# First four chunks' query and key products moved to head layout by TensorE selections, first six chunks' heads placed in the MLP's layout in PSUM

## The chip, the cores and the metric

The kernel runs on one core of a Trainium2 chip. The metric is the device time of one execution, in microseconds, from the first to the last instruction of the program and what lies around them. A core has TensorE (PE in the profile; PEld is its weight load), VectorE (DVE), ScalarE (ACT), GpSimd (POOL), SyncE (SP), whose queue starts all DMA transfers here, and 16 DMA engines. Matmuls write to PSUM, which has eight banks of 512 float32 columns.

## What is computed

Three parts follow one another: an attention in the form of a complex linear recurrence, a first MLP, and a second, gated MLP, all in float32.

```python
# q, k, v, a_re, a_im: (4, 8, 768, 48): batch, heads, sequence, head width
mag = sqrt(a_re**2 + a_im**2); scale = minimum(mag, 0.999) / (mag + 1e-6)
for t in range(768):                       # S is complex, 48 x 48 for each head
    S = a[t][:, None] * S + outer(k[t], v[t])
    y[t] = q[t] @ real(S)
x = y as (3072, 384)                       # token, head * 48 + column
g = log(1 + exp(x @ w_in)); x = g @ w_out  # 384 -> 2048 -> 384
out = ((x @ w1) * (x @ w2)) @ w3 @ w_out2  # 384 -> 1024 -> 1024 -> 384
```

Weights arrive as 64-bit numbers and are turned into float32 on the chip.

## The kernel before

**Chunks.** The 3072 tokens are cut into 24 chunks `u` of 128 tokens, six to a batch entry; `j` is a chunk's number within its entry. A chunk is worked on with features across the partitions: 384 features are G = 3 groups of 128 partitions, and head `h` takes features 48h to 48h + 47, so that heads 2 and 5 straddle two groups. `norm` (line 451) limits the size of `a`; `scan` (line 516) forms running products of `a` over pairs of chunks, in `P`; `inv` (line 576) forms the query product (`qkp(u, 0, ...)`) and the key product (`qkp(u, 1, ...)`), complex, in one tile `qkp` that has one buffer.

**From groups to heads.** The matmuls of the attention need each head's 48 features on partitions of their own, real parts on 0 to 47 and imaginary parts on 64 to 111: the tile `rs`, one for even and one for odd chunks. Step `s6` of `inv` (line 602) gets there through DRAM: it stores `qkp` to `pd[u]` and loads two halves of it back.

**Heads.** `mm` (line 615) does the rest of a chunk: `kt` turns the key products (transposes `ktp`, copied to `kT`), `sc` makes the scores of four heads in one PSUM bank (masked by VectorE into `am`), and `heads` (line 641) the outputs: `yp` takes, for each head, the state of the chunk before (`S` with `rs`; not where `j` is 0) and the present chunk (`v` with `am`), 48 columns wide, an even head on PSUM partitions 0 to 47 and an odd one on 64 to 111. `stp` is the new state. Two ScalarE copies bring `yp` to a tile `y`, which has one buffer.

**To the MLP's layout.** The MLP wants 384 features on KC = 3 tiles of 128 partitions, full to the last. The array `ROW` (line 65) gives each feature its row: heads 0 to 5 stay where they are, two to a tile, and the 48 columns of heads 6 and 7 fill the free partitions 48 to 63 and 112 to 127 of the three tiles, 16 columns each. Six small DMAs `y<-y` move these columns. Step `x` (line 680) then copies `y` to the block's input `xh` (and its rest to `xl`), or to `x` for the first two blocks.

**Blocks.** The first MLP runs over blocks of tokens: block 0 is chunk 0, block 1 chunks 1 and 2, block 2 chunks 3 to 5, and each later block three chunks. A block has 16 steps `f`: `s1` (line 850) makes `s` from `x`, ScalarE and VectorE make `g` from it, and `s2a` adds it into three banks `acc`. Blocks 0 and 1 use float32 weights, which arrive as raw pieces `wr` from `wio` (`w_load`, line 771; two loads to a piece) and are converted by ScalarE (`wtop`) and VectorE (`w_piece`, line 789) while block 0 runs. Later blocks use the weights and inputs split in two parts (`ww..h`, `ww..l`, `xh`, `xl`). Ahead of all this, `early` multiplies two weights of the second MLP (`wpa`, from `w3t` and `wo2`). Chunks of the next block are interleaved with the steps of a block. The second MLP (`pa`, `pb`, `bg`) follows when all blocks are done.

**PSUM.** Three banks are `acc`; the other five (`S1B = ATT = 5`, `ATAG = "s1"`) are shared by `s`, `ktp`, `sc`, `yp`, `stp` and others.

**Order.** Nothing is run as written: every operation is recorded by `Plan` (from line 79) with a cost and a latency, and `flush` (line 314) sorts them all by list scheduling, forwards and backwards in 16 rounds, one of them with noise from a fixed seed, and takes the best round. Each engine then works through its own list in that order; so does SP with the DMAs. `together` (line 225) keeps a group of matmuls in one piece. All recorded operations carry line 202 in the profile, and are told apart by their tiles.

Of the kernel before, what the change touches and what calls it, by code (L numbers as in the profile page):

```python
# [11 lines left out]
F32 = mybir.dt.float32  # L12
# [10 lines left out]
P = 128  # L23
B, H, SEQ, D = 4, 8, 768, 48
DM = H * D
NT = B * SEQ
T = 128
NCH = NT // T
CPB = SEQ // T
G = DM // P  # L30
# [3 lines left out]
KC = DM // P  # L34
NB = 384
# [5 lines left out]
HB = 5  # L41
# [4 lines left out]
YB = 1  # L46
VB = 1
# [9 lines left out]
CVS = 10  # L57
LEAD = 0
RATE = 340
ROUNDS = 16  # L60
SEED = 214
NBA = NT // NB
# [15 lines left out]
class Plan:  # L78
# [50 lines left out]
    def cost(self, eng, op, outs, ins):  # L129
        n = max(self.free_size(x) for x in (*outs, *ins))  # L130
        if eng == "SP":
            size = 2 if outs[0].dtype == I16 else 4
            for _, n in outs[0].ap:
                size *= n
            rate = 270 if hasattr(ins[0].tensor, "tag_meta") else RATE
            cost = max(650 if n < 512 and self.on_chip(ins[0]) else 475, size / rate)
# [177 lines left out]
    def flush(self):  # L314
# [15 lines left out]
        noise, best = Random(SEED), None  # L330
        for i in range(ROUNDS):
            start, _ = self.run(after, before, dict.fromkeys(before, 0.0), key, {})
# [25 lines left out]
def fused(ctx: ExitStack, tc: tile.TileContext, a_in, qk_in, v_in, wio, w12, w3t, wo2, q, k, v, a_re, a_im, outT):  # L358
    nc = tc.nc
    plan = Plan(tc)  # L360
    V, A, PE, GP, SP = plan.V, plan.A, plan.PE, plan.GP, plan.SP
# [15 lines left out]
    sp = fast.enter_context(tc.tile_pool(name="sp", bufs=2))  # L377
    ps = fast.enter_context(tc.tile_pool(name="ps", bufs=1, space=PSUM))
    ap = fast.enter_context(tc.tile_pool(name="ap", bufs=1))
# [3 lines left out]
    ident = cp.tile([P, P], F32, name="ident")  # L383
# [4 lines left out]
        out=mask, in_=mask, compare_op=ALU.is_ge, fill=0.0, base=0, pattern=[[1, T]], channel_multiplier=-1  # L388
# [23 lines left out]
    c = [dict() for _ in range(NCH)]  # L412
# [7 lines left out]
    def pst(tag, bufs, shape, name):  # L420
        return ps.tile(shape, F32, tag=tag, bufs=bufs, name=name)

    def att_ps(shape, name):
        return pst(ATAG, ATT, shape, name)
# [14 lines left out]

    def load_v(u):  # L440
        s = c[u]
        s["v"] = ap.tile([P, DM], F32, tag="v", bufs=VB, name=f"v{u}")
        SP.dma_start(s["v"], v_in[u])

    def half(u):
        return c[u // R]["P"][:, :, :, (u % R) * T : (u % R + 1) * T]

    def gt(x):
        return x.rearrange("p (g t) -> p g t", t=T)
# [112 lines left out]
    def qkp(u, i, f):  # L562
# [4 lines left out]
            op=ALU.mult,  # L567
        )

    rsw = [ap.tile([P, H * 2 * T], F32, tag=f"rs{i}", name=f"rs{i}") for i in range(2)]  # L570
    rs = [t[0 : 64 + D].rearrange("p (h q t) -> p h q t", h=H, q=2) for t in rsw]
    kT = ap.tile([P, H, 64 + D], F32, tag="kT", name="kT")
# [3 lines left out]
    def inv(u):  # L576
        s = c[u]

        def s1():
            s["n2"] = ap.tile([P, 2, GT], F32, tag="n2", name=f"n2{u}")  # L580
            A.activation(out=s["n2"].rearrange("p c (g t) -> p c g t", t=T), in_=half(u), func=AF.Square)

        def s2():
            n = s["n2"]
            V.tensor_tensor(out=n[:, 0], in0=n[:, 0], in1=n[:, 1], op=ALU.add)
            if u % CPB == CPB - 1:
                A.copy(pend[:, u // CPB], gt(n[:, 0])[:, :, T - 1])
            A.activation(out=n[:, 1], in_=n[:, 0], func=AF.Ln, bias=eps_p)
            A.activation(out=n[:, 1], in_=n[:, 1], func=AF.Exp, scale=-1.0)

        def s3():
            s["qkp"] = ap.tile([P, 2, G, 2, T], F32, tag="qkp", bufs=QKB, name=f"qkp{u}")
            qkp(u, 0, s["qk"][:, 0])

        def s4():
            n = s["n2"]
            V.tensor_tensor(out=n[:, 0], in0=n[:, 1], in1=s["qk"][:, 1], op=ALU.mult)

        def s5():
            qkp(u, 1, s["n2"][:, 0])  # L600

        def s6():
            s["rs"] = rs[u % 2]
            SP.dma_start(
                pd[u].rearrange("(m p) n -> p m n", p=P), s["qkp"].rearrange("p c g q t -> p (c g) (q t)")
            )
            for ri in range(2):
                SP.dma_start(
                    s["rs"][ri * 64 : ri * 64 + D].rearrange("d h q t -> d h (q t)"),
                    pd[u][ri * DM : (ri + 1) * DM].rearrange("(h d) n -> d h n", d=D),  # L610
                )

        return [s1, s2, s3, s4, s5, s6]

    def mm(u):
        s = c[u]
        j = u % CPB
        steps = []

        def kt(ri):  # L620
            def f():
                pt = att_ps([P, G, P], f"ktp{u}_{ri}")
                for g in range(G):
                    PE.transpose(pt[:, g], s["qkp"][:, ri, g, 1], ident)
                A.copy(kT[:, :, 64 * ri : 64 * ri + D], pt.rearrange("p g n -> p (g n)").rearrange("p (h d) -> p h d", d=D))

            return f

        def sc(hh):
            def f():  # L630
                pt = att_ps([P, 4, T], f"sc{u}_{hh}")
                for i in range(4):
                    h = hh * 4 + i
                    PE.matmul(pt[:, i], s["rs"][:, h, 1], s["rs"][:, h, 0], start=True, stop=True)
                am = ap.tile([P, 4, T], F32, tag="am", bufs=AMB, name=f"am{u}_{hh}")
                s[f"am{hh}"] = am
                V.tensor_tensor(out=am, in0=pt, in1=mask.unsqueeze(1).to_broadcast([P, 4, T]), op=ALU.mult)

            return f

        def heads(state):

            s["yp"] = att_ps([P, H // 2, T], f"yp{u}")
            pt = att_ps([P, DM], f"stp{u}") if state else None
            with plan.together():
                for pr in range(H // 2):
                    for prev in (True, False) if j else (False,):
                        for r in range(2):
                            h = 2 * pr + r
                            e = slice(h * D, (h + 1) * D)  # L650
                            w, m = (c[u - 1]["S"], s["rs"][:, h, 0]) if prev else (s["v"], s[f"am{h // 4}"][:, h % 4])
                            PE.matmul(
                                s["yp"][64 * r : 64 * r + D, pr], w[:, e], m,
                                start=prev or j == 0, stop=not prev,
                            )
                for h in range(H if state else 0):
                    for ri in range(2):
                        PE.matmul(
                            pt[64 * ri : 64 + D * ri, h * D : (h + 1) * D], kT[:, h, 64 * ri : 64 + D * ri],
                            s["v"][:, h * D : (h + 1) * D], start=True, stop=True,  # L660
                        )
            s["y"] = ap.tile([P, H // 2, T], F32, tag="y", bufs=YB, name=f"y{u}")
            for r in range(2):
                A.copy(s["y"][64 * r : 64 * r + D], s["yp"][64 * r : 64 * r + D])
            for k in range(KC):
                for r in range(2):
                    SP.dma_start(
                        s["y"][64 * r + D : 64 * (r + 1), k],
                        s["y"][64 * r + 16 * k : 64 * r + 16 * (k + 1), KC],
                    )  # L670
            if not state:
                return
            pt = pt[0 : 64 + D]
            s["S"] = ap.tile([64 + D, DM], F32, tag="S", bufs=2, name=f"S{u}")
            if j == 0:
                A.copy(s["S"], pt)
            else:
                V.tensor_tensor(out=s["S"], in0=pt, in1=c[u - 1]["S"], op=ALU.add)

        def x():  # L680
            bi, c0 = block_of(u)
            if c0 == 0:
                if bi < NATIVE:
                    xt[bi] = (sp.tile([P, KC, NB], F32, tag="xh", bufs=XB, name=f"x{bi}"), None)
                else:
                    xt[bi] = tuple(
                        sp.tile([P, KC, NB], F32R, tag=t, bufs=XB, name=f"{t}{bi}") for t in ("xh", "xl")
                    )
            d = slice(c0, c0 + T)
            xh, xl = xt[bi]  # L690
            if bi < NATIVE:
                A.copy(xh[:, :, d], s["y"][:, 0:KC])
            else:
                split(xh[:, :, d], xl[:, :, d], s["y"][:, 0:KC])

        steps = []
        if j < CPB - 1:
            steps += [kt(0), kt(1)]
        steps += [sc(0), sc(1), lambda: heads(j < CPB - 1), x]
        return steps  # L700

    att_end = {}
    groups = []
    u = 0
# [6 lines left out]
    for us in groups:  # L711
        n = len(us)
# [245 lines left out]
    for bi in range(nblk):  # L958
        last = bi == nblk - 1
        t0, n = BLOCKS[bi]  # L960
        if not last:
            start = att_pos[0]
# [87 lines left out]
    for bi in range(NBB):  # L1050
        gq = {}
        for f in range(FB):
# [6 lines left out]
            while ncheck[0] < min(NCK, NCK * it // nit):  # L1059
                src, n = cks[ncheck[0]]  # L1060
                r = raw3(src, n, f"ckr{ncheck[0]}")
# [4 lines left out]
    for i, n in enumerate(("min", "max")):  # L1066
        V.tensor_reduce(
            out=wlim[:, i : i + 1], in_=bst[n], axis=mybir.AxisListType.X, op=getattr(ALU, n)
        )
    okp = ap.tile([P, DM], F32, tag="v", bufs=VB, name="okp")  # L1070
    c0 = 0
    for src, lim, op in (
# [5 lines left out]
        n = src.shape[1]  # L1078
# [243 lines left out]
```

## Time and profile before

| | us |
|---|---|
| median of three executions | 947.0 (946.98 to 948.58) |
| profiled execution | 949.9 |
| its span, first to last instruction | 948.2 |
| TensorE busy in it | 889.4 (94%) |
| VectorE busy | 729.9 (77%) |
| ScalarE busy | 538.5 (57%) |
| GpSimd busy | 6.8 (1%) |

Busy times are read against the stretch that they lie in: an engine can be full in one stretch and have room in the next. In a profile line, `out<-in` are tiles without their numbers; a matmul of float32 has two instructions; `[4.0 <-ACT xh]` is idle time of the engine ahead of an instruction and what ended it. PEclk is the granted clock of TensorE: 1.00 is 2.4 GHz and 0.50 is 1.2 GHz.

### The profile page before, as it was taken

The page shows a single profiled execution, that of the slowest core. Times are in us where ns is not written, and L with a number is a line of the kernel's source. Part 1 is how long each engine was busy: PE and PEld are TensorE (multiplying, and loading weights), DVE is VectorE, ACT ScalarE, POOL GpSimd, SP SyncE. Part 2 cuts the span into 40 slices and gives each one's busy share as a digit, 9 for nine tenths or more (in the row PEclk, how much of TensorE's full clock was granted, in tenths as well). Part 3 has the DMA queues.
Part 4 walks back from the last instruction along what each step waited for, and adds up shares of the span by engine and source line. Part 5 has one row for each costly group of instructions (what it writes and reads, how often), then busy time and mean ns, then how long its engine had stood idle before and what let it go on. Part 6 is the DMA issues. An engine that isn't in the chain of part 4 may idle for free.

```text
span 948.2 us, 15624 instructions
## 1 busy us (share of the span) xinstructions
PE 889.4 (94%) x5673; PEld 800.3 (84%) x5673; DVE 729.9 (77%) x1591; ACT 538.5 (57%) x1096; POOL 6.8 (1%) x15
## 2 busy tenths in 40 slices
PE   3957779989999999999999999999999999999996
PEld 2536768889999999999999999998878787888885
DVE  6899889999999999899989755599888786222221
ACT  6566885678687689587785655773221323231322
POOL 2000000000000000000000000000000000000000
PEclk9986889999999999999999999999999999999999
DMA  9999866154737455563654435247787774000001
GB/s 346 324 280 279 252 184 146 55 148 113 164 101 153 121 128 114 134 161 61 191 135 130 119 96 132 76 136 243 236 261 237 242 230 145 1 33 1 34 1 37
DMA packets 89127, 141.74 MB, mean 149 GB/s; under 512 B 8273, under 2 KB 60625, under 8 KB 89041
## 3 DMA queue, kind: packets, MB, share of 16 engines
q1 hardware_dynamic: 89040, 140.66, 52.8%
q8 instruction: 46, 0.75, 0.3%
q14 instruction: 41, 0.33, 0.1%
HBM read 109.56 MB, written 29.88 MB: 147 GB/s over the span
## 4 chain that ended last, share of the span: by engine, by line
PE 69%; DMA 13%; DVE 11%; ACT 3%; issue 3%; SPq 1%; DVEq 0%; ACTq 0%
PE acc L202 25%; PE s L202 20%; PE pa L202 6%; PE pb L202 6%; PE sc L202 4%; PE yp L202 3%; DMA ckr<-w3t 3%; DMA ckr<-wio 3%; DMA wr<-wio 3%; DVE ck L202 2%; PE wpa L202 2%; DMA pd<-qkp 2%; DVE P L202 2%; PE stp L202 1%; DVE tm L202 1%
## 5 line engine op out<-in xcount | busy, mean ns | idle before, releaser
L202 DVE TENSOR_TENSOR tm<-P 128x90 f32<-128x90 f32 (+3 forms) x240 | 144.6, 616 | 1.5
L202 ACT ACTIVATE e<-e 128x384 f32<-128x384 f32 (+2 forms) x288 | 135.8, 487 | 2.7
L202 DVE TENSOR_TENSOR bg<-pa,bg 128x512 f32<-128x512 f32 x48 | 33.0, 688 | 91.8 <-PE pa L202 81.5
L202 ACT ACTIVATE e<-s 128x384 f32<-128x384 f32 (+2 forms) x144 | 64.6, 451 | 54.0 <-PE s L202 50.8
L202 ACT CAST bgg<-bg 128x512 fp32r<-128x512 f32 x48 | 29.8, 621 | 114.7 <-DVE bg L202 114.7
L202 DVE SCALAR_TENSOR_TENSOR g<-s,e 128x384 f32<-128x384 f32 (+2 forms) x144 | 73.6, 515 | 24.5 <-ACT e L202 24.4
L202 DVE TENSOR_TENSOR P<-tm 128x45 f32<-128x45 f32 (+11 forms) x304 | 87.2, 344 | 1.6
L202 ACT COPY bg<-pb 128x512 f32<-128x512 f32 x48 | 28.2, 587 | 85.2 <-PE pb L202 78.4
L202 DVE TENSOR_TENSOR gl<-g,gh 128x384 fp32r<-128x384 f32 x112 | 62.1, 559 | 5.8 <-ACT gh L202 5.1
L202 ACT CAST gh<-g 128x384 fp32r<-128x384 f32 x112 | 56.7, 507 | 16.1 <-DVE g L202 11.5
L202 PE MATMUL sc<-rs 112*128 112x128 f32 x384 | 55.1, 286 | 7.3 <-DMA rs<-pd 7.3
L202 PEld LDWEIGHTS sc<-rs 112*128 112x128 f32 x384 | 53.2, 201 | 8.7 <-issue 7.8
L202 DVE CUSTOM_DVE_ANT_0 ck<-ckr 128x384 f32<-128x384 f32 x80 | 43.4, 542 | 21.6 <-DMA ckr<-w3t 9.7
L202 PE MATMUL wpa<-wo,w 128*128 128x384 f32 x128 | 43.2, 499 | 14.3 <-DVE w L202 14.3
L202 PE MATMUL s<-x,w 128*128 128x128 f32 (+1 forms) x192 | 40.8, 363 | 13.7 <-ACT x L202 8.2
L202 PE MATMUL acc<-bgg,bwp0h 128*128 128x512 f32 x144 | 50.8, 391 | 1.7 <-ACT bgg L202 1.3
L202 PEld LDWEIGHTS wpa<-wo,w 128*128 128x128 f32 x128 | 24.9, 196 | 31.5 <-DVE w L202 14.5
L202 PE MATMUL acc<-bgg,bwp2h 128*128 128x512 f32 x144 | 49.2, 392 | 1.2 <-DVE bgg L202 0.8
L202 PEld LDWEIGHTS s<-x,w 128*128 128x128 f32 x192 | 33.7, 218 | 17.5 <-ACT x L202 8.6
L202 DVE TENSOR_TENSOR bgg<-bg,bgg 128x512 fp32r<-128x512 f32 x48 | 33.0, 688 | 16.3 <-ACT bgg L202 16.3
L202 DVE TENSOR_REDUCE lims<-ck 128x1 f32<-128x384 f32 x80 | 43.1, 538 | 2.3
L202 PE MATMUL yp<-am,v 128*48 128x128 f32 x384 | 36.3, 279 | 2.0 <-ACT nt L202 2.0
(372 smaller groups left out, 2308.5 us busy)
## 6 DMA issues: line engine op xcount, KB each, us to landing
pd<-qkp SPq DMA_DIRECT2D x24, 768.0 KB, 4.5
rs<-pd SPq DMA_DIRECT2D x48, 384.0 KB, 6.2
ckr<-wio SPq DMA_DIRECT2D x32, 384.0 KB, 3.8
wr<-wio SPq DMA_DIRECT2D x32, 383.8 KB, 7.3
a<-a_in SPq DMA_DIRECT2D x24, 384.0 KB, 3.7
qk<-qk_in SPq DMA_DIRECT2D x24, 384.0 KB, 3.8
w12r<-w SPq DMA_DIRECT2D x16, 384.0 KB, 3.3
ckr<-w SPq DMA_DIRECT2D x16, 384.0 KB, 3.6
```

The costliest lines, as they stand in the source:

```text
L202: getattr(engine.unit, op)(*args, **kw)
```

## The change

For chunks 0 to 3 (`PICK = 4`), the trip of the query and key products through DRAM gives way to matmuls with selection matrices. `picks` holds, for each head and each group that it lies in (10 pairs), a 128 x 64 matrix of zeros and ones, cut from the identity. `pick(i)` multiplies the query (i = 0) or key (i = 1) product with them, the real part to PSUM partitions 0 to 63 and the imaginary part to 64 to 127, four heads to a bank, and ScalarE copies partitions 0 to 111 to `rs`. It is called as soon as the product in question is there.

For chunks 0 to 5 (`PLACE = 6`), the matmuls of `yp` write the MLP's layout at once. `v` now holds heads 0 to 5 padded with zeros to 64 columns each, then heads 6 and 7 (480 columns instead of 384, for all chunks). For tile k and half r, a first matmul writes 64 rows from head 2k + r; a further one, with weights `ext` of 64 columns whose first 48 are zero and whose last 16 are columns 16k to 16k + 15 of head 6 + r, adds the other head's columns to the rows 48 to 63. The same is done for the state's part where there is one (`ext[1]`, from `S`). ScalarE fills the 16 columns of `ext` for each chunk. `y` is then the PSUM tile itself, and the two copies and the six moves fall away. From chunk 6 on the old way stays, with `vcols` naming the padded columns. `ext` and `picks` lie in buffers of the tiles `gh` and `gl`, which block 2 is the first to use otherwise.

```diff
+PICK = 4
+PLACE = 6
+VW = 6 * 64 + 2 * D
...
-        s["v"] = ap.tile([P, DM], F32, tag="v", bufs=VB, name=f"v{u}")
+        s["v"] = ap.tile([P, VW], F32, tag="v", bufs=VB, name=f"v{u}")
...
+    ext = [sp.tile([P, NB], F32, tag="gh", bufs=HB, name=f"ext{i}") for i in range(2)]
+    for t in ext:
+        GP.memset(t, 0.0)
+    ext = [t.rearrange("p (r k n) -> p r k n", r=2, k=KC) for t in ext]
+    picks = [sp.tile([P, NB], F32, tag="gl", bufs=HB, name=f"pick{i}") for i in range(2)]
+    sels = {}
+    for i in range(2):
+        GP.memset(picks[i], 0.0)
+    for h in range(H):
+        for g in range(h * D // P, ((h + 1) * D - 1) // P + 1):
+            p0 = max(h * D, g * P)
+            n = min((h + 1) * D, (g + 1) * P) - p0
+            i, c0 = divmod(len(sels) * 64, NB)
+            sels[h, g] = picks[i][:, c0 : c0 + 64]
+            GP.tensor_copy(
+                out=picks[i][:, c0 + p0 - h * D : c0 + p0 - h * D + n], in_=ident[:, p0 - g * P : p0 - g * P + n]
+            )
...
+        def pick(i):
+            s["rs"] = rs[u % 2]
+            for hh in range(2):
+                pt = att_ps([P, 4, T], f"pk{u}_{i}_{hh}")
+                with plan.together():
+                    for n in range(4):
+                        h = 4 * hh + n
+                        gs = [g for g in range(G) if (h, g) in sels]
+                        for ri in range(2):
+                            for g in gs:
+                                PE.matmul(
+                                    pt[64 * ri : 64 * ri + 64, n], sels[h, g], s["qkp"][:, ri, g, i],
+                                    start=g == gs[0], stop=g == gs[-1],
+                                )
+                A.copy(s["rs"][:, 4 * hh : 4 * hh + 4, i], pt[0 : 64 + D])
...
+        if u < PICK:
+            return [s1, s2, s3, lambda: pick(0), s4, s5, lambda: pick(1)]
         return [s1, s2, s3, s4, s5, s6]
...
+            if u < PLACE:
+                A.copy(
+                    ext[0][:, :, :, D:],
+                    s["v"][:, 384:VW].rearrange("p (r k n) -> p r k n", r=2, k=KC),
+                )
+                if j:
+                    A.copy(
+                        ext[1][0 : 64 + D, :, :, D:],
+                        c[u - 1]["S"][:, 6 * D :].rearrange("p (r k n) -> p r k n", r=2, k=KC),
+                    )
             with plan.together():
-                for pr in range(H // 2):
+                for k in range(KC if u < PLACE else 0):
+                    for r in range(2):
+                        h = 2 * k + r
+                        lo = s["yp"][64 * r : 64 * r + 64, k]
+                        PE.matmul(lo, s["v"][:, h * 64 : (h + 1) * 64], s[f"am{h // 4}"][:, h % 4], start=True, stop=False)
+                        if j:
+                            PE.matmul(
+                                lo[0:D], c[u - 1]["S"][:, h * D : (h + 1) * D], s["rs"][:, h, 0], start=False, stop=False
+                            )
+                            PE.matmul(lo, ext[1][0 : 64 + D, r, k], s["rs"][:, 6 + r, 0], start=False, stop=False)
+                        PE.matmul(lo, ext[0][:, r, k], s["am1"][:, 2 + r], start=False, stop=True)
+                for pr in range(H // 2 if u >= PLACE else 0):
...
-            s["y"] = ap.tile([P, H // 2, T], F32, tag="y", bufs=YB, name=f"y{u}")
-            for r in range(2):
+            if u < PLACE:
+                s["y"] = s["yp"]
+            else:
+                s["y"] = ap.tile([P, H // 2, T], F32, tag="y", bufs=YB, name=f"y{u}")
+            for r in range(2 if u >= PLACE else 0):
                 A.copy(s["y"][64 * r : 64 * r + D], s["yp"][64 * r : 64 * r + D])
-            for k in range(KC):
+            for k in range(KC if u >= PLACE else 0):
                 for r in range(2):
                     SP.dma_start(
```

## Rows read from the trace of the kernel before

**Rows 1.** The page: busy tenths in 40 slices of 23.7 us, TensorE and VectorE.
```profile
PE   3957779989999999999999999999999999999996
...
DVE  6899889999999999899989755599888786222221
```

**Rows 2.** By stretch: length, busy us (x instructions) by engine, PEclk, DMA share, GB/s.
```profile
52.00:132.60 80.60, 53.12 (x457) 48.36 (x455) 74.18 (x164) 60.06 (x129) 0.00 (x0) 0.79 0.86 248
132.60:194.50 61.90, 57.90 (x407) 50.81 (x407) 57.32 (x123) 41.11 (x95) 0.00 (x0) 0.97 0.48 117
...
195.00:330.00 135.00, 134.82 (x1055) 132.32 (x1055) 132.29 (x294) 101.09 (x217) 0.00 (x0) 0.99 0.55 135
330.00:592.00 262.00, 259.41 (x2061) 253.53 (x2060) 224.43 (x498) 189.02 (x408) 0.00 (x0) 1.00 0.53 128
```

**Rows 3.** Timeline, TensorE's waits: start, us, engine, line, operation, count [idle before <-releaser].
```profile
69.37 3.76 PE L202 MATMUL sc<-rs 112*128 112x128 f32 x16 [5.45 <-DMA rs<-pd]
...
132.61 2.93 PE L202 MATMUL s<-x,w 128*128 128x256 f32 x6 [5.51 <-ACT x L202]
...
194.47 1.10 PE L202 MATMUL s<-xh,ww0h 128*128 128x384 f32 x3 [3.99 <-ACT xh L202]
```

**Rows 4.** VectorE's waits, 52 to 194.5 us: who <- whom: us in total, times, longest.
```profile
DVE w L202 <- ACT wtop_wa L202: 3.2, 2, 2.4
...
DVE ww1l L202 <- PE acc L202: 1.4, 1, 1.4
```

**Rows 5.** DMA from 52 to 112 us: the sum, and issues (KB each, us to landing).
```profile
DMA packets 9604, 16.61 MB, mean 277 GB/s; under 512 B 750, under 2 KB 6070, under 8 KB 9599
...
wr<-wio SPq DMA_DIRECT2D x26, 383.8 KB, 8.0
pd<-qkp SPq DMA_DIRECT2D x3, 768.0 KB, 5.5
```

**Rows 6.** Timeline: SP's queue around chunk 0's moves, ScalarE's wait for a weight.
```profile
78.56 3.79 SPq L202 DMA_DIRECT2D y<-y  x6
82.39 7.45 SPq L202 DMA_DIRECT2D wr<-wio  x11
...
111.86 1.04 ACT L202 CAST wtop_wa<-wr 128x768 f16<-128x768 bf16 x1 [2.76 <-DMA wr<-wio]
```

**Rows 7.** TensorE's pace: chain of waits from 145 us, and weight loads at 164 us.
```profile
150.30 1.90 PE yp L202 x32
...
155.46 0.89 PE sc L202 x8
...
164.52 0.17 PEld L202 LDWEIGHTS yp<-rs,S 112*48 112x48 f32 x4 [0.33 <-DVE g L202]
```

**Rows 8.** Instructions by form, 107.0 to 107.36 us: the two halves of `stp`.
```profile
L202 PE MATMUL stp<-v,kT 128*48 128x48 f32 x9 | 0.6, 209 | 0.0
L202 PE MATMUL stp<-v,kT 128*64 128x48 f32 x7 | 0.6, 219 | 0.0
```

**Rows 9.** ScalarE's copies by form (`y` from 52 to 195 us): count | busy, mean ns.
```profile
L202 ACT COPY bg<-pb 128x512 f32<-128x512 f32 x48 | 28.2, 587 | 85.2 <-PE pb L202 78.4 <-DMA outT<-xob 4.9 <-DVE bgg L202 1.9
...
L202 ACT COPY y<-yp 48x512 f32<-48x512 f32 x12 | 7.0, 580 | 2.7 <-PE yp L202 2.2 <-DVE xl L202 0.3
...
L202 ACT COPY xoa<-acc 128x128 f32<-128x128 f32 x3 | 0.8, 259 | 0.0
```

**Rows 10.** Timeline, GpSimd's last work.
```profile
6.68 0.74 POOL L202 MEMSET wtop_wa<- 128x768 int32 x1
```

**Rows 11.** By stretch, those at half clock: the last, and the sum of all five.
```profile
194.80:198.10 3.30, 3.30 (x12) 3.30 (x11) 3.30 (x7) 1.10 (x2) 0.00 (x0) 0.50 0.91 319
sum 40.40, PE 25.80 PEld 24.03 DVE 37.85 ACT 23.59 POOL 0.00; mean PE 5.16 PEld 4.81 DVE 7.57 ACT 4.72 POOL 0.00
```

**Rows 12.** Timeline of ScalarE at the end of chunk 5.
```profile
186.01 1.19 ACT L202 COPY y<-yp 48x512 f32<-48x512 f32 x2 [2.19 <-PE yp L202]
...
193.92 0.49 ACT L202 CAST xh<-y 128x384 fp32r<-128x384 f32 x1
```

More of the change, by code (lines that the diff above doesn't have):

```diff
@@ L568, in qkp, with vcols @@
         )
+    def vcols(h):
+        return slice(h * 64, h * 64 + D) if h < 6 else slice(384 + (h - 6) * D, 384 + (h - 5) * D)
+    ext = [sp.tile([P, NB], F32, tag="gh", bufs=HB, name=f"ext{i}") for i in range(2)]
[15 more added lines that the diff above has]
+            )
     rsw = [ap.tile([P, H * 2 * T], F32, tag=f"rs{i}", name=f"rs{i}") for i in range(2)]
@@ L649, in heads @@
                             h = 2 * pr + r
-                            e = slice(h * D, (h + 1) * D)
                             w, m = (c[u - 1]["S"], s["rs"][:, h, 0]) if prev else (s["v"], s[f"am{h // 4}"][:, h % 4])
+                            e = slice(h * D, (h + 1) * D) if prev else vcols(h)
                             PE.matmul(
@@ L659, in heads @@
                             pt[64 * ri : 64 + D * ri, h * D : (h + 1) * D], kT[:, h, 64 * ri : 64 + D * ri],
-                            s["v"][:, h * D : (h + 1) * D], start=True, stop=True,
+                            s["v"][:, vcols(h)], start=True, stop=True,
                         )
-            s["y"] = ap.tile([P, H // 2, T], F32, tag="y", bufs=YB, name=f"y{u}")
-            for r in range(2):
+            if u < PLACE:
[3 more added lines that the diff above has]
+            for r in range(2 if u >= PLACE else 0):
                 A.copy(s["y"][64 * r : 64 * r + D], s["yp"][64 * r : 64 * r + D])
-            for k in range(KC):
+            for k in range(KC if u >= PLACE else 0):
                 for r in range(2):
@@ L1291, in cols, with pad @@
         return np.asarray(w).reshape(KC, P, -1, P).transpose(2, 1, 0, 3)
+    def pad(x):
+        x = x.reshape(NCH, T, H, D)
+        y = np.zeros((NCH, T, 6, 64), np.float32)
+        y[..., 0:D] = x[:, :, 0:6]
+        return np.concatenate([y.reshape(NCH, T, 384), x[:, :, 6:].reshape(NCH, T, 2 * D)], axis=2)
     def bits(w):
@@ L1299 @@
         "qk_in": np.concatenate([pack(q), pack(k)], axis=2),
-        "v_in": np.asarray(v).transpose(0, 2, 1, 3).reshape(NCH, T, DM),
+        "v_in": pad(np.asarray(v).transpose(0, 2, 1, 3).reshape(NCH, T, DM)),
         "wio": np.concatenate([cols(w_in[np.argsort(ROW)]).reshape(FA, P, DM), w_out.reshape(FA, P, DM)], axis=2),
```

## The prediction

> **What bounds the kernel now.** I read the page's 40 slices first. TensorE (PE) is at nine tenths or more from about 142 us to the end; before that it has holes, while VectorE (DVE) is nearly full from 50 to about 380 us [rows 1]. So whatever moves TensorE's dense part earlier moves the end, and whatever lengthens it moves the end too. The changed steps all lie between 52 us, where the weight products thin out, and 194.5 us, where block 2 starts; I cut the table by stretch there, with one more cut at 132.6 us, the start of block 1. In these 142.5 us TensorE works 53.1 + 57.9 = 111.0 us, VectorE 74.2 + 57.3 = 131.5 us, ScalarE (ACT) 101.2 us [rows 2]. From 195 to 330 us TensorE idles 0.2 us and VectorE 2.7 us; from 330 to 592 TensorE idles 2.6 us. A block 2 that starts earlier therefore carries the rest with it, one for one.
>
> The waits of TensorE name what the change aims at [rows 3]: 5.5 us for `rs`, the round trip of chunk 0 through DRAM; 5.5 us before block 1 and 4.0 us before block 2, each for a copy of `y` behind the moves `y<-y`. All of them are TensorE's, and VectorE, the fuller engine, has few idle times of its own [rows 4]: 3.2 us for weight pieces that the DMA brought late, 1.4 us for TensorE's `acc`, and small ones. VectorE has 142.5 - 131.5 = 11.0 us idle in all, and that is what the start of block 2 can gain as long as VectorE's work ahead of it stays what it is.
>
> **What is removed.** For chunks 0 to 3, one store to `pd` (768 KB) and two loads that read it back by halves: 1.57 MB a chunk. Three of these chunks fall between 52 and 112 us, where 16.6 MB move in all [rows 5]; 4.7 MB or 28% of that goes, and the last of the 26 loads of `wio`, for which ScalarE waits until 111.9 us [rows 6], can land earlier by up to 4.7 MB / 0.277 MB per us = 17 us. For chunks 0 to 5, six moves `y<-y` each: 36 issues on SP of some 0.6 us. SP works in order, and its queue shows the other cost: chunk 0's six moves stand at 78.6 us, and 11 loads of `wio` come only behind them, from 82.4 us. Two ScalarE copies of `y` a chunk go as well, 12 x 0.58 = 7.0 us.
>
> **What is added on TensorE.** A picked product has 10 matmuls for each of real and imaginary part, 20 for q and 20 for k, of 64 output columns, real to the lower and imaginary to the upper half of the array. The nearest row is `yp`: 32 instructions of 48 columns, two for a matmul, alternating between the halves, take 1.90 us, so 0.107 us a matmul, or 0.119 us with its entry; `sc`, with all columns, needs 0.89 / 4 = 0.222 us [rows 7]. The step into `yp` leaves the weight load idle for 0.33 us; I take 0.3 us for each of the 16 groups of picks (four a chunk). 160 x 0.107 + 16 x 0.3 = 21.9 us. If the halves did not overlap, 160 x 0.222 + 4.8 = 40.3 us. A lower end below 17.1 us is excluded, since `yp`'s pace is the fastest that a row shows for this length.
>
> Placing the heads makes 24 matmuls of 16 (12 of 8 in chunk 0, which has no state). New is their order: four in a row into the same half, then four into the other. In `stp` the program alternates halves, yet in the first 0.36 us 9 instructions of the upper half start beside 7 of the lower [rows 8]: the halves run at their own pace, so a row of four can overlap the next. I take 24 / 16 x 1.90 = 2.85 us plus 0.4 us of tail, 1.35 us more than now, for chunks 1 to 5, and 0.45 us for chunk 0: 7.2 us. Not overlapped it would be 24 x 0.222 - 1.90 = 3.4 us a chunk, 18.8 us in all; the low end is 4.9 us, without tails. Added on TensorE: 29.1 us, between 22 and 59 us.
>
> The Trainium skill speaks against this order: "TensorE: Matmul & The Clock Gate", Part 3 (The mechanism), says that matmuls start and end strictly in program order and only weight loads are pulled ahead. By that rule eight matmuls in runs of four take six steps instead of four, and the added work would be the 35.7 us of a rival below; the count in `stp` disagrees with it.
>
> **What is added elsewhere.** ScalarE: 16 copies of 512 columns out of PSUM at 0.587 us and 11 small ones of 96 columns, near the 0.26 us of 128 columns, 9.4 + 2.9 - 7.0 = 5.3 us more [rows 9], under 41 us of idle time. Without that cover it would be 5.3 us on the path. The heads' PSUM bank is now held until VectorE has read it for `xl`, about 1 us more by the length of the copies, and longer when VectorE is late: zero while one of the five shared banks is free, and up to that wait on TensorE when none is; I take zero. GpSimd gets 4 fills and 10 small copies; a fill of twice the width takes 0.74 us now [rows 10], and its queue is empty from 7.4 us, 40 us before the first pick. They cost nothing unless they stand ahead of `wtop`, and then up to some 6 us at the very start. Loads of `v` grow by a quarter, 0.05 MB a chunk: 0.2 us each of DMA, under the relief above.
>
> **The sum.** TensorE: of its 111.0 us, 25.8 - 3.3 = 22.5 us ran at 1.2 GHz (granted clock 0.50) in four stretches that follow holes [rows 11]. At 2.4 GHz that is 11.2 us less, so 99.8 us. With 29.1 us added: 128.9 us, 13.6 us under the 142.5 us. VectorE needs 131.5 us. Hence VectorE sets the earliest start, 183.5 us, and TensorE comes close behind, at 180.9 us without any hole. Of VectorE's 11.0 us idle I let the two waits go whose cause is removed, the weight pieces (3.2 us) and the late block 1 (1.4 us), and 1.9 us among the small ones: 6.5 us. The other 4.5 us stay. Block 2 then starts at 188.0 us. That fits chunk 5's end: its heads are done at about 186 us, and the copies, the moves and ScalarE's queue hold `xh` back until 193.9 us [rows 12]; read straight out of PSUM it needs no more than the 0.5 us copy. What is late next is VectorE, with the scans of the following chunks.
>
> So the span goes from 948.2 to 941.7 us. The profiled execution took 949.9 us, 1.7 us outside its span, and is 2.9 us above the median of 947.0; the median goes to 947.0 - 6.5 = 940.5 us.
>
> **The rivals.** (a) More gain: VectorE puts work for chunks 6 and later behind block 2's start, and TensorE sets it at 181 us: -13.5 us, 933.5. For it: block 2 needs chunks up to 5 alone, and the norms and scans run two to three chunks ahead of that. Against: from there to 330 us VectorE has 2.7 us to spare to catch up in.
> (b) No change: VectorE's idle time stays, because its inputs come from its own chains; the filled TensorE holes are then hidden anyway, 947. For it: VectorE is at nine tenths or more all the way to block 2 and past it [rows 1]. Against: two of its waits have a cause that is removed.
> (c) The halves hold to program order: a picked product takes 11 steps of 0.214 us instead of 10, the picks 23.6 us, a placed chunk 19 steps or 4.1 us, the places 12.1 us: 35.7 us, so TensorE needs 135.5 us. With 5 us of holes left, as in the wait for chunk 0's products at about 60 us, block 2 starts at 192.5 us: 945. This is the rule named above.
> (d) Slower: TensorE's new work takes the place of the wait inside block 1. If block 1 still starts at 132.6 us, since VectorE was busy 74.2 of the 80.6 us ahead of it, TensorE has to put chunk 3's picks (5.5 us) and three placed chunks (4.05 us) into a stretch with 4.0 us of room: +5.5 us, 952.5. It decides as soon as block 1 starts later than 127.1 us. Against: the wait for `y` just before block 1 is 5.5 us alone, and the loads of weights come earlier.
>
> **How the numbers follow.** Forecast 0.54, (a) 0.12, (b) 0.10, (c) 0.06, (d) 0.18. The forecast itself reaches from 936 to 945: 4 us either way for the VectorE waits that stay, and the order beyond 330 us, which is planned anew, can win or lose about the 2.6 us of holes there. For 8 in 10, the range takes in most of (a) and of (d): 932 to 951, with the unoverlapped halves (59 us, block 2 not before 210 us) left out. About 0.2% (1.9 us) is what a measurement of this kernel can tell from no change. Faster: 0.54 + 0.12 + half of (c) = 0.69; same: (b) and half of (c), 0.13; slower 0.18.
>
> **What would show it.** Right: block 1 starts by 123 to 128 us, block 2 at 184 to 192 us without a hole ahead of it; the picks take about 1.4 us a group and a placed chunk 3.2 us; VectorE idles 4 to 6 us from 52 us to block 2; the piece of `wio` at 112 us comes by 100 us. Wrong: the picks or placed heads at 0.2 us a matmul, a hole before block 2, VectorE's idle time as now, or the time lost again behind 195 us.

## The result, and the profile after

The change takes the median from 947.0 to 933.6 us (four executions, 931.2 to 935.2): a ratio of 0.9855 [0.9829, 0.9882], or 13.4 us less. The sign is the forecast one, and the size is twice the 6.5 us forecast. It is the time of rival (a), 933.5 us, which had the chance 0.12; how much of that is chance is said further down.

The page of the changed kernel (operations now carry line 205). TensorE stands at nine tenths from the second slice on, where before it did so from 142 us, but for the eight tenths of the slice in which block 2 began [rows 1], and the granted clock at nine tenths or more in every slice:

```profile
span 931.2 us, 16377 instructions
...
PE 905.4 (97%) x6081; PEld 815.5 (88%) x6081; DVE 727.6 (78%) x1591; ACT 540.6 (58%) x1111; POOL 12.2 (1%) x29
...
PE   3999999999999999999999999999999999999997
...
DVE  6999999999999899999989855599888785231221
...
PEclk9999999999999999999999999999999999999999
```

By stretch, in the columns of [rows 2]; block 1 now starts at 119.4 us (before 132.6) and block 2 at 183.5 us (before 194.5):

```profile
0.00:52.00 52.00, 37.85 (x110) 22.20 (x111) 42.84 (x88) 33.51 (x50) 12.20 (x29) 1.00 0.92 330
52.00:119.40 67.40, 67.05 (x800) 60.68 (x799) 65.27 (x147) 61.01 (x141) 0.00 (x0) 1.00 0.61 216
119.40:183.50 64.10, 62.39 (x481) 55.53 (x480) 62.25 (x136) 42.00 (x100) 0.00 (x0) 1.00 0.42 106
52.00:183.50 131.50, 129.44 (x1278) 116.21 (x1277) 127.52 (x281) 103.00 (x239) 0.00 (x0) 1.00 0.52 162
183.50:319.00 135.50, 135.09 (x1064) 132.24 (x1063) 134.51 (x302) 102.56 (x222) 0.00 (x0) 1.00 0.57 137
319.00:592.00 273.00, 270.72 (x2118) 263.59 (x2117) 228.80 (x504) 195.77 (x424) 0.00 (x0) 1.00 0.51 128
```

From 52 us to block 2 TensorE idled 142.5 - 111.0 = 31.5 us before, and idles 131.5 - 129.4 = 2.1 us now. Its waits over the whole span (who <- whom: us in total, times, longest) are the first one, on weights at the start, which stood before too, and then crumbs. The waits for `rs`, `x` and `xh` of [rows 3] are gone:

```profile
PE wpa L205 <- DVE w L205: 14.2, 1, 14.2
PE yp L205 <- DVE am L205: 1.7, 1, 1.7
PE acc L205 <- ACT gh L205: 0.8, 1, 0.8
PE s L205 <- DVE g L205: 0.6, 2, 0.4
PE sc L205 <- DVE am L205: 0.6, 1, 0.6
PE s L205 <- ACT xh L205: 0.5, 1, 0.5
```

The starts of block 1 and block 2 in the timeline, where no wait stands behind either line, and ScalarE's last conversion of a weight. Before, it waited for a piece until 111.9 us [rows 6], and its last conversion came at 117.7 us; SP issued the last load of `wio` at 104.4 us, and does so at 83.6 us now:

```profile
96.73 1.05 ACT L205 CAST wtop_ws<-wr 128x768 f16<-128x768 bf16 x1
...
119.37 1.46 PE L205 MATMUL s<-x,w 128*128 128x256 f32 x6
...
183.54 0.79 PE L205 MATMUL s<-xh,ww0h 128*128 128x384 f32 x3
```

And the new work by form: the picks' 320 instructions (two to a matmul), 16 groups of 1.30 us, and ScalarE's copies of them:

```profile
L205 PE MATMUL pk<-qkp,pick 128*64 128x128 f32 x320 | 20.8, 278 | 0.0
...
L205 ACT COPY rs<-pk 112x512 f32<-112x512 f32 x16 | 9.3, 582 | 3.5 <-PE pk L205 3.5
```

**The account.** A span is TensorE's busy time plus its idle time. Before: 889.4 + 58.8 = 948.2. After: 905.4 + 25.8 = 931.2, of which 14.2 us idle lie ahead of 52 us in both. Busy time grew by 16.0 us: by some 29.8 us of new work (picks 20.8; five placed chunks at 3.57 us instead of 1.90; about 0.6 for chunk 0), less 12.9 us, an estimate, since the 25.8 us at half clock [rows 11] now run at 2.4 GHz; that is 16.9, and some records can be missing. Idle time fell by 33.0 us. The two profiled executions thus differ by 17.0 us; the medians by 13.4, since before's stood 2.9 us above its median and after's 0.7 below.

By place, 10.9 of the 17.0 us come from the start of block 2. The other 6.0 come behind it, from there to the end: 753.7 us before, 747.7 now.

### The profile page after: what moved, and what is told of

It reads as the page before. It is cut to its first block, busy times and chain, and to the rows that moved or that the text cites. A ratio compares the mean times of both kernels' runs of the same rounds, so it can differ in the third digit from the quotient of the medians.

```text
span 931.2 us, 16377 instructions
## 1 busy us (share of the span) xinstructions
PE 905.4 (97%) x6081; PEld 815.5 (88%) x6081; DVE 727.6 (78%) x1591; ACT 540.6 (58%) x1111; POOL 12.2 (1%) x29
## 4 chain that ended last, share of the span: by engine, by line
PE 81%; DVE 11%; DMA 4%; issue 1%; ACT 1%; SPq 1%; DVEq 0%; ACTq 0%
PE acc L205 28%; PE s L205 17%; PE pb L205 11%; PE pa L205 11%; PE yp L205 4%; PE wpa L205 3%; PE sc L205 3%; DVE tm L205 3%; DVE P L205 3%; DMA a<-a_in 2%; PE stp L205 1%; PE pk L205 1%; PE ktp L205 1%; DVE g L205 1%; DVE qkp L205 1%
## 5 line engine op out<-in xcount | busy, mean ns | idle before, releaser
L205 ACT CAST bgg<-bg 128x512 fp32r<-128x512 f32 x48 | 29.8, 621 | 104.2 <-DVE bg L205 104.2
L205 PE MATMUL wpa<-wo,w 128*128 128x384 f32 x128 | 44.6, 509 | 14.2 <-DVE w L205 14.2
L205 PE MATMUL sc<-rs 112*128 112x128 f32 x384 | 52.2, 276 | 0.7 <-DVE am L205 0.6
L205 PEld LDWEIGHTS sc<-rs 112*128 112x128 f32 x384 | 49.6, 191 | 2.7 <-DVE g L205 0.9
L205 PE MATMUL yp<-am,v 128*48 128x128 f32 (+1 forms) x360 | 40.9, 277 | 0.0
L205 PE MATMUL acc<-g,w 128*128 128x128 f32 (+1 forms) x192 | 38.5, 331 | 0.0
L205 DVE TENSOR_TENSOR am<-sc,mask 128x512 f32<-128x512 f32 x48 | 33.5, 697 | 6.4 <-PE sc L205 5.7
```

The costliest lines, as they stand in the source:

```text
L205: getattr(engine.unit, op)(*args, **kw)
```

## The experiments

Each run has the ratio to the kernel before on the same chip, with its 95% interval. Idle is the profiled span less TensorE's busy time.

| kernel | median us | ratio | TensorE busy + idle = span | block 1, block 2 from |
|---|---|---|---|---|
| before | 947.0 | | 889.4 + 58.8 = 948.2 | 132.6, 194.5 |
| after | 933.6 | 0.9855 [0.9829, 0.9882] | 905.4 + 25.8 = 931.2 | 119.4, 183.5 |
| after_again | 932.9 | 0.9861 [0.9829, 0.9893] | 905.3 + 26.0 = 931.3 | 118.0, 182.1 |
| place_only | 939.7 | 0.9945 [0.9923, 0.9967] | 891.1 + 44.7 = 935.8 | 125.6, 186.4 |
| pick_only | 934.2 | 0.9883 [0.9846, 0.9921] | 898.1 + 34.7 = 932.8 | 118.9, 175.9 |
| before_s7 | 949.4 | 1.0038 [1.0024, 1.0053] | 890.1 + 57.9 = 948.0 | 135.2, 192.7 |
| after_s7 | 934.6 | 0.9895 [0.9862, 0.9928] | 903.7 + 27.9 = 931.6 | 117.9, 182.5 |
| pe_more | 946.0 | 1.0009 [0.9994, 1.0023] | 915.5 + 28.0 = 943.5 | 125.4, 193.2 |
| dve_more | 935.0 | 0.9886 [0.9854, 0.9919] | 905.2 + 27.5 = 932.7 | 120.6, 181.2 |
| pp_3_6 | 933.9 | 0.9888 [0.9850, 0.9926] | 900.4 + 30.8 = 931.2 | 117.0, 178.0 |
| pp_4_3 | 938.1 | 0.9915 [0.9886, 0.9944] | 903.4 + 32.6 = 936.0 | 117.3, 178.0 |
| bytes_back | 934.6 | 0.9879 [0.9855, 0.9904] | 906.3 + 26.6 = 932.9 | 120.4, 181.0 |
| packets_back | 935.7 | 0.9899 [0.9865, 0.9933] | 906.3 + 27.1 = 933.4 | 120.8, 181.3 |
| picks_idle | 951.7 | 1.0057 [1.0022, 1.0093] | 904.3 + 45.7 = 950.0 | 133.5, 195.8 |
| halves | 933.8, one execution | | 906.5 + 25.5 = 932.0 | 118.5, 184.2 |
| alt | 931.0 | 0.9843 [0.9817, 0.9868] | 903.5 + 25.3 = 928.8 | 118.8, 182.4 |
| alt_s7 | 931.4 | 0.9852 [0.9821, 0.9883] | 901.1 + 28.6 = 929.7 | 115.7, 178.5 |

Two theories were tested. The **VectorE theory** is the prediction's own: VectorE sets the start of block 2, and the rest follows one for one. The **TensorE theory** is rival (a) thought through: with its holes filled TensorE is the bound all the way, and the time is its work plus the holes that are left. An expectation gives its theories letters of its own; from pe_more on, A is the VectorE theory and B the TensorE theory.

### The two parts, one at a time

```diff
-PICK = 4
+PICK = 0
```

> The change with its placed heads alone (PICK = 0). Theory A, the start of block 2 sets the time and both parts bring it forward: the waits for the moves of y before blocks 1 and 2 (5.5 and 4.0 us) go, the trip of the products through DRAM stays, so block 1 starts at about 127 us, block 2 at 189 to 191 us, and the time falls by 3 to 6 us, to 941 to 944. Theory B, the new order of the whole program is by chance a better one: no sum of the parts need hold, and this lies anywhere from 935 to 952.

```diff
-PLACE = 6
+PLACE = 0
```

> The change with its picked products alone (PLACE = 0). Theory A: the wait for rs (5.5 us) and the late weights go, block 1 starts by 122 us, but 4 us of wait for y stay before block 2, which starts at 187 to 191 us; the time falls by 4 to 8 us, to 939 to 943. With the placed heads alone it adds up to about the whole 13.4 us. Theory B: anywhere from 935 to 952.

Placing alone gains 0.55%, picking alone 1.2%, both 1.4 to 1.45%: less than the sum of 1.7%, though the intervals do not exclude the sum. Theory A held for place_only in time (5.2 us by the ratio; block 2 came earlier than the 189 to 191 us that it gave) and missed pick_only, in time (11.1 us) and in block 2, which was to start at 187 to 191 us. In place_only TensorE still waits 4.0 us for `x` and 3.8 us for `rs<-pd`. In pick_only block 2 starts at 175.9 us, earlier than in any other run of the table, after this wait:

```profile
175.89 0.79 PE L205 MATMUL s<-xh,ww0h 128*128 128x384 f32 x3 [3.02 <-ACT xh L205]
```

Yet it takes 934.2 us, no less than the whole change with block 2 at 183.5. The stretch ahead of it (in the columns of [rows 2]) shows VectorE with 0.3 us idle, and 123.6 us of work where 131.5 were to be fixed:

```profile
52.00:175.90 123.90, 119.21 (x1173) 106.74 (x1168) 123.56 (x275) 103.44 (x232) 0.00 (x0) 1.00 0.56 172
```

Of the 7.9 us left out there, 2.3 are done ahead of 52 us (43.9 us of VectorE's work there, 41.6 before); most of the rest stands behind block 2's start, among it the step `tm` of a later chunk's scan (1.8 us) and a product `qkp` (1.0 us). So that start is no measure of the end, and VectorE's work ahead of it no constant. Placing on top of picking adds 7.3 us of TensorE's work and takes 8.9 us of its idle time; the two intervals overlap, so whether it gains anything on top is not settled.

### The order planned anew

Any change gives another order of the whole kernel, and this could have been the gain. Another noise for the planner, in both kernels, and the change once more:

```diff
-SEED = 214
+SEED = 7
```

> The kernel before with another seed of the planner's noise, so another order of the same work. Theory A: within 3 us of 947, with TensorE idle 25 to 32 us between 52 us and block 2, as before. Theory B: the orders of one program differ by as much as the change did, 8 us or more, and some of it behind block 2.

> The changed kernel with the same other seed. Theory A: 931 to 938, block 2 at 182 to 188 us. Theory B: back to 940 or later.

> The changed kernel itself, for comparison on the same chip: 933.6 us, some 12 to 13 us under the kernel before.

Another order moves the kernel before by +0.4% and the change by about as much, and with the second order the change gains 949.4 - 934.6 = 14.8 us. The gain is not one order's luck, but differences of about 0.4% between single kernels of the table may be.

### More work for one engine

TensorE: picking matmuls of chunks 2 and 3 made twice.

```diff
                         for ri in range(2):
-                            for g in gs:
...
+                            for rep in range(2 if u in (2, 3) else 1):
+                                for g in gs:
```

> The changed kernel with every picking matmul of chunks 2 and 3 issued twice in its group: 80 matmuls more on TensorE, 80 x 0.107 = 8.6 us, nothing else. Theory A, VectorE sets the start of block 2 and the rest follows: TensorE has 2 us of room ahead of block 2 (129.4 of 131.5 us), so the time rises by 6 to 7 us if they land there, and block 2 moves by as much. Theory B, TensorE's own work sets the time and VectorE's work gives way: +8 to +9 us.

VectorE: the query and key products of chunks 0 to 3 made twice.

```diff
     def qkp(u, i, f):
-        V.tensor_tensor(
...
+        for rep in range(2 if u < 4 else 1):
+            V.tensor_tensor(
```

> The changed kernel with the eight products of chunks 0 to 3 made twice on VectorE: 8 x 0.96 = 7.7 us more work of VectorE, all of it needed before the scores of these chunks. Theory A: VectorE has 4.0 us of idle time ahead of block 2 (127.5 of 131.5 us), so block 2 starts 4 to 8 us later and the time rises by as much. Theory B: VectorE puts other work behind block 2, whose start moves by less than 3 us, and the time rises by 0 to 2 us.

By form, the repeated matmuls (first line) and products (the other two; eight more than the 48 of the change):

```profile
L205 PE MATMUL pk<-qkp,pick 128*64 128x128 f32 x480 | 32.9, 278 | 0.0
```

```profile
L205 DVE TENSOR_TENSOR qkp<-P,qk 128x768 f32<-128x768 f32 x28 | 27.2, 971 | 0.3
L205 DVE TENSOR_TENSOR qkp<-P,n 128x768 f32<-128x768 f32 x28 | 27.1, 969 | 0.3 <-PE ktp L205 0.3
```

32.9 - 20.8 = 12.1 us more on TensorE, where 8.6 were expected, cost 13.1 us against after_again, in the same comparison: one for one. By itself this does not part the theories, since A too would give 12.1 - 2.1 = 10 us. 8 x 0.97 = 7.8 us more on VectorE, all ahead of block 2, cost 2.1 us; the intervals overlap, and by the time alone up to some 7 us are possible, which theory A would allow. What ends the VectorE theory is the start of block 2: it was to come 4 to 8 us later, and came at 181.2 us, 0.9 earlier than in after_again and 2.3 earlier than in the change. From the span's start to block 2, here and in the change (VectorE is the third pair of numbers):

```profile
0.00:181.20 181.20, 165.63 (x1383) 137.40 (x1383) 172.25 (x372) 134.23 (x285) 12.60 (x29) 1.00 0.64 210
```

```profile
0.00:183.50 183.50, 167.29 (x1387) 138.40 (x1388) 170.37 (x368) 136.51 (x288) 12.20 (x29) 1.00 0.63 210
```

172.3 us with 7.8 us of repeats leave 164.5 us where the change has 170.4. Among what now stands behind the start of block 2 are three splits of weights that block 2 itself needs only in its later steps; the change makes all three ahead of it, the last (`ww8l`) at 167.1 us:

```profile
187.20 1.00 DVE L205 TENSOR_TENSOR ww6l<-w,ww6h 128x768 fp32r<-128x768 f32 x1
...
196.44 0.97 DVE L205 TENSOR_TENSOR ww7l<-w,ww6h 128x768 fp32r<-128x768 f32 x1
...
203.67 0.95 DVE L205 TENSOR_TENSOR ww8l<-w,ww8h 128x768 fp32r<-128x768 f32 x1
```

Behind the start VectorE has room: 273.0 - 228.8 = 44 us from 319 to 592 us in the change.

### Less of each part

```diff
-PICK = 4
+PICK = 3
```

> The changed kernel with three picked chunks instead of four: 5.2 us less on TensorE (four groups of 1.30 us), and chunk 3's products go through DRAM again, off the path as long as they have some 20 us. Theory A: no change, since VectorE sets block 2. Theory B: 3 to 5 us faster than the changed kernel, unless chunk 3's trip turns into a wait of TensorE.

```diff
-PLACE = 6
+PLACE = 3
```

> The changed kernel with the heads placed for chunks 0 to 2 only. Theory B: 3 x 1.27 = 3.8 us less on TensorE, and the wait for y before block 2 is back (3.0 us with the picks alone, and some 1.7 us at 1.2 GHz behind it): within 2 us of the changed kernel. Theory A: 2 to 5 us slower than the changed kernel, as block 2 waits again.

One chunk's picks less takes 5 us off TensorE's work and starts block 2 some 5 us earlier, and gives 5.0 us back as idle time, 1.6 of them in the wait for the first weights: the same end. Theory A, no change, has the number here but not the start of block 2, which it holds fixed. It shows the limit of the TensorE theory: less work helps only where no hole opens. Three placed chunks less cost 4.5 us against the change, where theory B allowed 2 and theory A said 2 to 5, and again block 2 starts earlier (178.0 us) instead of later. TensorE has 2.0 us less work and 6.8 us more idle time: the waits for `xh` are back with 5.2 us in all, and 3.1 us for a `g`. It is slower even than none placed (pick_only), with intervals that overlap, so a part of this may be the order.

### What the trip through DRAM cost: bytes, packets or the waiting

The trip's bytes are put back with nothing waiting for them, in four copies of 384 KB a chunk:

```diff
+        def traffic():
+            for t in tr[u]:
+                for m in range(2):
+                    SP.dma_start(t[m], qk_in[u].rearrange("p c n -> p (c n)").rearrange("p (m x) -> (p m) x", x=256))
```

> The changed kernel with four copies of 393 KB from DRAM to DRAM, in rows of 1 KB, for each of chunks 0 to 3, issued behind the key product, for which nothing waits: the bytes of the trip are back, its wait is not. Theory C, the picks gain by the bytes that they save, since the weights of block 0 land earlier: block 1 starts 5 to 12 us later than in the changed kernel, with holes on TensorE, and the time rises by 4 to 9 us. Theory D, they gain by the wait alone: under 2 us.

The same with the rows apart, so that packets stay at 1 KB:

```diff
+                    SP.dma_start(t[m][:, 0 : 2 * T], qk_in[u].rearrange("p c n -> p (c n)").rearrange("p (m x) -> (p m) x", x=256))
```

> As bytes_back, but each row of 1 KB lands apart from the next, so that the DMA engines get as many packets of 1 KB back as the trip had (some 3000 to 4500 more from 52 to 112 us). Theory C, the load on the DMA engines is what the picks take away: the last weight is converted after 105 us instead of 94 to 98, and the time rises by 4 us or more over the changed kernel. Theory D, the wait is: under 2 us.

And pick_only with the trip kept behind the picks: it writes the same values to `rs` once more, so that all waits of the trip are back beside the picks' work.

```diff
-            return [s1, s2, s3, lambda: pick(0), s4, s5, lambda: pick(1)]
+            return [s1, s2, s3, lambda: pick(0), s4, s5, lambda: pick(1), s6]
```

> The picked products alone, as in pick_only, with the trip through DRAM kept behind them, which writes the same values into rs again: the picks' cost without their gain, 20.8 us on TensorE and 9.4 us on ScalarE. Theory B: against the kernel before, TensorE's holes and its time at 1.2 GHz (44.6 us idle behind the start, 13 us lost to the clock) take most of it, and the time lies 0 to 8 us above the kernel before; the removed trip is then worth 11 to 19 us. If nothing hides them, 966 us.

The sum of the DMA from 52 to 112 us: the change, then packets_back, which moves more bytes and packets than the kernel before [rows 5]:

```profile
DMA packets 5500, 14.01 MB, mean 233 GB/s; under 512 B 609, under 2 KB 1387, under 8 KB 5492
```

```profile
DMA packets 10695, 19.35 MB, mean 322 GB/s; under 512 B 824, under 2 KB 6461, under 8 KB 10687
```

Its last weight is converted at 94.2 us all the same (93.9 in bytes_back), so the added traffic does not hold up the weights. The time is 1 to 2 us above the change in bytes_back and 2 to 4 in packets_back, with intervals that overlap. So the bytes are a small part of the trip's cost; by the intervals, though, the packets could cost up to some 8 us. In picks_idle the last weight is converted at 120.2 us (97.7 in pick_only), SP issues the last load of `wio` at 111.5 us (84.4 in pick_only, 83.4 in packets_back), and these are the waits of its SP queue (40 to 120 us) and of TensorE (52 to 186 us):

```profile
SPq L205 <- DMA pd<-qkp: 6.7, 3, 3.8
...
PE sc L205 <- DMA rs<-pd: 6.1, 1, 6.1
PE s L205 <- ACT x L205: 2.6, 2, 1.5
PE sc L205 <- DVE g L205: 2.6, 1, 2.6
PE s L205 <- DVE w L205: 1.9, 1, 1.9
```

The trip is worth 1.0057 - 0.9883, or 16.5 us, beside the same picks, with some 5 us either way by the intervals. What it costs is in the main waiting: SP stands behind a store that has yet to land, the loads of weights queue behind SP, and TensorE waits for `rs` and `w`. How the 16.5 us divide between SP's queue and the direct wait for `rs` was not tried. The picks themselves, about 20 us of TensorE's work, cost picks_idle only 5.4 us against the kernel before: TensorE is busy 14.9 us longer and idle 13.1 us less, at a mean granted clock of 0.991 where before had 0.977 to 0.984, so the rest of them fell into holes and stretches at half clock.

### The order of the placed matmuls

Runs of four in one half (chunks 1 and 5), alternating halves (2 and 4), and twelve of one half, then twelve of the other (3):

```diff
+                if u in (2, 4):
+                    line = [x for k in range(KC) for pair in zip(runs[2 * k], runs[2 * k + 1]) for x in pair]
+                elif u == 3:
+                    line = [x for r in range(2) for k in range(KC) for x in runs[2 * k + r]]
+                else:
+                    line = [x for h in range(2 * KC) for x in runs[h]]
```

> The changed kernel with the placed matmuls in three orders: chunks 1 and 5 four to a half in turn, as in the change, chunks 2 and 4 alternating between the halves, chunk 3 twelve for the lower half and then twelve for the upper. Theory E, the halves run at their own pace with a short queue: four in a row 3.2 us, as measured, alternating 2.8 to 3.0 us, twelve in a row 4.5 to 5 us. Theory F, strict program order: four in a row 4.1 us, alternating 2.8 us, twelve in a row 5.2 us.

The stretches around chunks 1, 2 and 3, with `yp` alone (length, TensorE's busy us and instructions, then weight loads and the other engines):

```profile
86.00:92.00 6.00, 3.57 (x48) 3.33 (x48) 0.00 (x0) 0.00 (x0) 1.00 0.68 266
111.00:117.00 6.00, 2.85 (x48) 2.61 (x48) 0.00 (x0) 0.42 (x1) 1.00 0.23 77
130.00:137.00 7.00, 5.10 (x48) 4.85 (x48) 0.00 (x0) 0.48 (x1) 1.00 0.00 0
```

The same 24 matmuls take 2.85 us alternating, 3.57 in runs of four (not the 3.2 that the expectation calls measured) and 5.10 in two runs of twelve. Rival (c), strict program order, had 4.1 us for the runs of four. At a pace of its own for each half, all three would be near 2.85. Within a run an instruction starts every 0.11 us, so all 48, one behind the other, would take 47 x 0.11 + 0.27 = 5.4 us, an estimate from the timeline. Against that, five changes of half save 1.9 us and a single one saves 0.3: some 0.35 us at each. So the halves run apart, but only over a short way. The timelines show how far, in the change and in the runs of twelve: where the half changes, the first instruction of the new run (`v`) starts 0.33 us ahead of the last of the run before it (`ext`, with `am`), together with the fourth from its end, and not sooner:

```profile
113.13 0.27 PE L205 MATMUL yp<-rs,ext 112*64 112x128 f32 x1
113.13 0.32 PE L205 MATMUL yp<-am,v 128*64 128x128 f32 x1
...
113.46 0.27 PE L205 MATMUL yp<-am,ext 128*64 128x128 f32 x1
```

```profile
133.22 0.27 PE L205 MATMUL yp<-rs,ext 112*64 112x128 f32 x1
133.22 0.32 PE L205 MATMUL yp<-am,v 128*64 128x128 f32 x1
...
133.54 0.27 PE L205 MATMUL yp<-am,ext 128*64 128x128 f32 x1
```

So all placed chunks were put in alternating order (`if True:` in the place of the first condition above), and the same with the second noise:

> The changed kernel with all placed matmuls alternating between the halves. Theory B, TensorE's work sets the time: 0.2 to 0.4 us less for each of five chunks, 1 to 2 us faster than the changed kernel, at the edge of what can be told. Theory A: no change.

> The placed matmuls alternating between the halves, with the planner's other seed. Theory B: 1 to 3 us under the changed kernel with that seed (934.6), so 931 to 934. Theory A, or chance of the order: 934 to 937.

Chunk 1 now takes what chunk 2 took:

```profile
86.00:92.00 6.00, 2.85 (x48) 2.61 (x48) 0.00 (x0) 0.00 (x0) 1.00 0.79 312
```

Five chunks at 0.72 us are 3.6 us of TensorE's time, of which its busy time shows 1.9 and 2.6 us. The ratios are lower than the change's in both orders, 0.9843 to 0.9855 and 0.9852 to 0.9895, and the intervals overlap in both: a gain of 1 to 4 us, the same in sign twice and not settled in size. Alternating is the fastest version that was run.

## Why the prediction was right or wrong

**The step that failed** is "VectorE needs 131.5 us. Hence VectorE sets the earliest start, 183.5 us", and with it "one for one". The reservation stood in the text ("as long as VectorE's work ahead of it stays what it is") and was then taken as given. The evidence against it stood there too, in rival (a): block 2 needs chunks up to 5 alone, and norms and scans run two to three chunks ahead. In the change VectorE did 127.5 us instead of 131.5 in the stretch: 1.2 us more ahead of 52 us, some 2.8 us behind block 2. Two splits of weights that block 2 needs in its later steps show it, before and after:

```profile
175.06 0.95 DVE L202 TENSOR_TENSOR ww9l<-w,ww8h 128x768 fp32r<-128x768 f32 x1
...
188.09 1.00 DVE L202 TENSOR_TENSOR ww10l<-w,ww10h 128x768 fp32r<-128x768 f32 x1
```

```profile
186.71 1.00 DVE L205 TENSOR_TENSOR ww9l<-w,ww8h 128x768 fp32r<-128x768 f32 x1
...
192.29 0.99 DVE L205 TENSOR_TENSOR ww10l<-w,ww10h 128x768 fp32r<-128x768 f32 x1
```

Both stand ahead of block 2's start before (194.5 us) and behind it after (183.5 us). That with the idle time left is why block 2 starts at 183.5 and not at 188.0 us. That this is the very figure of the floor, 183.5 us, is chance: the floor had VectorE without idle time, and it idles 4.0 us. "One for one" fails by pick_only: block 2 starts 7.6 us earlier there than in the change, and the end is the same. The runs showed what to take in its place: TensorE's added work, less the holes that close, less the half clock, over the whole span.

**Where the other 6.9 us came from.** Block 2 started 4.5 us earlier than forecast. Behind it lie 6.0 us more: the half clock at 194.8 us [rows 11], 3.3 / 2 = 1.65 us, which the sum left out although the row was there; waits of 2.9 us for `bgg` in the second MLP, which the change's profile does not have, though after_again, the same kernel, has 1.9 us of them at the same span, so a part of this term is chance; and the rest, some 1.5 us, which no row names. Less the 3.6 us by which the profiled pair differs more than the medians, that is 6.9.

**Right in the sum.** TensorE from 52 us to block 2: 128.9 forecast, 129.4 measured. A group of picks: 1.37 and 1.30 us. The half clock: 22.5 us at half clock halved; the granted clock stays at 1.00 in every stretch from the start to 592 us now. VectorE's idle time to block 2: 4.5 and 4.0 us, and the waits for `w` and `ww1l` [rows 4] are gone. GpSimd's new work ends at 13 us and nobody waits for it. The stages named as what is late next, VectorE's scans, were not.

**Sizes that were off.** A placed chunk takes 3.57 us where 3.25 were forecast: "the halves run at their own pace" held for a short look ahead only. The cost is 5 x 0.3 = 1.6 us. The sum did not suffer, since the picks were 1.1 us cheaper. The other size is the relief of the weights' loads: SP's last load of `wio` was issued 20.8 us earlier and the last weight converted 20.9 us earlier, where 17 at most had been worked out from the bytes. What was relieved is the queue and not the bytes, as packets_back shows.

**The rivals.** (a) gave the time and named the cause, work of VectorE that moves behind block 2's start; but in the change that is in part block 2's own splits of weights, not only work for chunks 6 and later. That it hits the time to 0.1 us is luck: it had block 2 at 181 us and all of the 13.5 us from there, where 10.9 us came from there and 6.0 from behind, less the 3.6 us of the profiled pair. (b) fell with the result; VectorE was not at nine tenths all the way either, since the two slices from 95 to 142 us stand at eight [rows 1]. (c): the Trainium skill, "TensorE: Matmul & The Clock Gate", Part 3 (The mechanism), has matmuls start and end in program order; the trace of this case disagrees: a chunk in runs of four takes 3.57 us where (c) had 4.1, and in runs of four as of twelve the first matmul of the next half starts 0.33 us ahead of the last of the run before it. (d) was to decide from a block 1 later than 127.1 us; it started at 119.4. Its mechanism is real all the same: in pe_more, with no hole left, TensorE's work costs its full length, and 12 us of it take the whole gain away.

## What to carry to other kernels

Where two engines are both nearly full, as here, write the span as busy plus idle of each and ask which of the two has work that can move past the stage's end; the other one is the bound. An edit that puts work on the bound engine pays as long as it closes more of that engine's holes than it adds, and once the holes are gone the next microsecond of work costs a microsecond. A round trip that an in-order queue has to wait for costs more than its bytes: here it held up the loads that stood behind it in the queue by some 27 us (111.5 against 84.4 us for the last), beside the wait for its own result.

## What had not been expected of the hardware

Matmuls into the two column halves of the array start out of program order, but only 0.33 us ahead, so they overlap only where the order of issue changes halves: 2.85 us alternating, 3.57 in runs of four and 5.10 in runs of twelve for the same 24. The repeats in pe_more would fit in, though no run tried it for them: where a half gets two to four matmuls in a row instead of one or two, an added instruction costs 12.1 / 160 = 0.076 us, against 20.8 / 320 = 0.065 us on average in the change.
